# Two decoder layers for one token on one core: 256 more floats of W_q stay in SBUF for layer two

## The chip, the core and the metric

The kernel runs on one core of one Trainium2 chip. The metric is device time in microseconds (us) of one execution. Three executions of the kernel before gave a median of 729.7 us (729.67 to 729.95).

## The reference

Two identical layers share their weights and caches. Each layer is attention followed by a gated MLP, with a layer norm ahead of each and a residual sum behind each. There are 4 batches, one query token, a width of 640, 32 heads of 128, and of each cache the last W = 1024 positions count.

```python
W = min(4096, max(256, Sk // 4))
q = (x @ wq).reshape(B, Sq, Hq, Dh).transpose(0, 2, 1, 3)
k = k_cache[:, :, Sk - W:, :]
v = v_cache[:, :, Sk - W:, :]
scores = jnp.einsum("bhqd,bhkd->bhqk", q, k) * (Dh ** -0.5)
o = jnp.einsum("bhqk,bhkd->bhqd", softmax(scores), v)
# ... attention: o.transpose(0, 2, 1, 3).reshape(B, Sq, Hq * Dh) @ wo
gate, up = x @ W_gate, x @ W_up          # 640 -> 1728
h = gate * (gate > 0) * up               # then h @ W_down, 1728 -> 640
# ...
x = x + attention(layernorm(x)); x = x + mlp(layernorm(x))   # twice
```

All data are float32. One layer reads 10.5 MB of W_q, 67 MB of K, 67 MB of V, 10.5 MB of W_o and 13.3 MB of MLP weights.

## The kernel before

The weights and caches are laid out in HBM as three long rows of 128 partitions, in the order in which the program reads them: `heads` (the heads that are streamed in each layer), `kept` (five heads, which layer one reads last and which stay in SBUF for layer two), and `mlp`. A fourth, `limbs`, holds 512 floats of one head's V (head 17) cut into short pieces of 5 or 2 or 1 rows, which fill partitions of a small region at the end of SBUF.

SBUF holds the tile `store` of 50304 floats a partition and the tile `first_q`, which holds the first HELD = 4608 floats of `heads` (the beginning of W_q) from the start to the end, so that layer two does not load them again. A list `plan`, written out before anything is issued, says for each load the layer, the row, the range and the place in `store`. `load()` walks along it on SyncE (SP): a load is issued as soon as every column of its place is free, and nothing behind it goes first. `done` marks columns free after the matmuls that read them. So the order of the loads is fixed by `plan`, and the moment at which one may start is set by TensorE (PE), which reads the place's last data. Under each `dma_start` the wait stands on SP's own queue.

The stages, and what sets the order in each:

- Layer one's attention goes over groups of four heads (the last ones of three and two): `query` multiplies by W_q, `query_turned` transposes into `qT`, `scores` accumulates K products in the PSUM tile `ps`, `softmax` makes `probs`, `values` accumulates V products in `po` with weights in the two tiles `pT`, `project` adds W_o products to `y`. Loads there have up to MOST = 16064 floats a partition, and go round in three thirds of `store`.
- At the end of layer one's attention the kept heads fill `store` up to FRONT = 47360. Layer one's MLP has to pass through a small ring: what is left behind FRONT, plus three ranges of kept data that are parked elsewhere for a while: AHEAD (1088 floats of W_q, parked in free columns of `probs` and in the two `pT`), BACK (1728 floats of V, parked in `ps`, in columns 128 to 511 of `po` and in the tile of `y`), AWAY (1280 more floats of V, parked in `pp` and the two PSUM banks `m`). The ring has 7040 floats in seven places.
- `forward` is the MLP: `gate(j)` for the four parts 3, 0, 1, 2 (accumulating in one of the two halves of the PSUM tile `pp`), `gated(j)` (Relu on ScalarE (ACT), the product on VectorE (DVE)), `hidden(j)` (a transpose) and `down(j)` into `y`. In layer one `fill` and `busy` issue matmuls on the identity into `po[:, :P]` whose result nobody reads; they stand among the real ones.
- Layer two starts with the kept heads, then streams `heads` from column HELD on, first into the ring's places and then into larger and larger ones, and ends with `mlp` in pieces that grow smaller.

The layer norm is `normalized` (mean, subtraction, sum of squares with its ACT `accum_out`, transpose into `xT`) and `deviation` (four small matmuls for the variance, square root on ACT, reciprocal on DVE). `query_out` applies the reciprocal to the query's product on DVE.

Loads are L229 (`first_q`), L242 (rows of 128 partitions) and L238 (limbs). All products with loaded data are issued by the helper `product` (L276). L358 is `busy`, L365 is `fill`, L374 the sums over partitions in `mean`, L425 `query_out`, L605 and L606 `gated`.

Of the kernel before, what the change touches and what calls it, by code (L numbers as in the profile page):

```python
# [14 lines left out]
P = 128  # L15
# [44 lines left out]

HELD = 4608
STORE = 50304
FRONT = KEPT * 2 * (D + KV)


AHEAD = KEPT * D, KEPT * D + 1088
INSIDE = 864
BACK = FRONT - 2 * KV - 1728, FRONT - 2 * KV
AWAY = BACK[0] - 1280, BACK[0]
HOME = 12864  # L70
FIRST, MOST = 32128, 16064
LAP = 3 * MOST
SPLIT, PART = 17, 2048
LIMBS = [(half + i, 5, 0, 1536) for i in range(4) for half in (0, 32)] + [(i, 2, 1536, PART) for i in range(3)] + [(3, 1, 1536, PART), (7, 1, 1536, PART)]
RUNS = [(half, 20, 512 * s, 40 * s + 20 * (half > 0)) for s in range(3) for half in (0, 32)] + [(0, 8, 1536, 120)]
# [38 lines left out]
def decode_kernel(ctx: ExitStack, tc: tile.TileContext, x, source, out):  # L114
# [29 lines left out]
    def stretch(layer, lo, end, to):  # L144

        loads = []
        for hi in fewest(lo, end, -(-(end - lo) // MOST))[1]:
            if to + hi - lo > LAP:
                to = 0
            loads.append((lo, hi, to))  # L150
            to, lo = to + hi - lo, hi
        last = next(i for i, (lo, hi, _) in enumerate(loads) if lo < at_part("v", SPLIT) + KV - 512 <= hi)
        for i, (lo, hi, at) in enumerate(loads):
            if last - 3 < i <= last:
                half = (i - last + 1) * 6 + 1
                plan.extend((layer, "limbs", p, p + 1, STORE - PART) for p in range(max(half, 0), half + 6))
            put(layer, "heads", at, lo, hi)
        return to
# [19 lines left out]
    put(0, "heads", q_end, turn, *mid, heads_end)  # L178
    put(0, "kept", k0, k0, k1, v0, v0 + 6656, v1, v1 + KV, v1 + 7168, FRONT)
    put(0, "kept", 0, 0, len(HEADS[K0]) * D, KEPT * D)  # L180


    f, z, a, q, k = FRONT, STORE - D, AHEAD[0], AWAY[0], BACK[0]
    assert STORE - FRONT == 1280 + 1024 + D
    gu = [(z, D), (f, 1280), (f + 1280, 1024), (a, 1088), (k, 960), (k + 960, 768), (q, 1280)]
    gu_end = [(f, 1280), (f + 1280, 1024), (z, D), (a, D + 256)]
    wd = [(k, 960), (k + 960, D), (q, 1280), *gu_end, (k, D), (k + D, D)]
    lo = 0
    for to, n in gu + gu + gu_end + wd:
        put(0, "mlp", to, lo, lo + n)  # L190
        lo += n
    assert lo == MLP


    lo = HELD
    for to, n in (f, 1280), (f + 1280, 1024), (z, D), (a, 1088), (k, 1728):
        put(1, "heads", to, lo, lo + n)
        lo += n
    to = AHEAD[1]
    for n in 832, 1280, 1024, 2048, 3392:  # L200
        to = put(1, "heads", to, lo, lo + n)
        lo += n
# [12 lines left out]
    for lo, hi in (last, near(last + 12800)), (near(last + 12800), heads_end):  # L215
        to = put(1, "heads", to if to + hi - lo <= STORE else 0, lo, hi)
    cuts = [0, 7040, 12160, GU0 + 3 * GU, WD1 + WD, MLP - 4 * D, MLP - 2 * D, MLP - D, MLP - QUARTER, MLP]
    for lo, hi in zip(cuts, cuts[1:]):
# [32 lines left out]
    def place(layer, row, lo):  # L251
# [4 lines left out]
        if row == "kept" and layer:  # L256
            if AHEAD[0] <= lo < AHEAD[1]:
                i = lo - AHEAD[0] - INSIDE
                if i < 0:
                    return probs, 1024 + i, -i  # L260
                return pT[i // P], GAP + i % P, min(P - i % P, AHEAD[1] - lo)
            if BACK[0] <= lo < BACK[1]:
# [144 lines left out]

    def query(layer, g, spread=False):

# [12 lines left out]
        part_done(layer, "q", g, c * n, n)  # L422

    def query_out(g, rstd):
# [38 lines left out]
    def values(layer, g, last=False):  # L463
# [30 lines left out]
        if last:  # L494
# [4 lines left out]
            if layer == 0:  # L499
                nc.gpsimd.tensor_copy(pT[0][:, GAP:], store[:, AHEAD[0] + INSIDE:AHEAD[0] + INSIDE + P])  # L500
                rest = AHEAD[1] - AHEAD[0] - INSIDE - P
                nc.vector.tensor_copy(pT[1][:, GAP:GAP + rest], store[:, AHEAD[1] - rest:AHEAD[1]])
                free(*AHEAD)
# [31 lines left out]
    def attention(layer):  # L535
        gs = order[layer]
        rstd = deviation(normalized())
        table(AF.Exp)
        query(layer, gs[0], True)
        if layer:  # L540
            for t in pT:
                nc.gpsimd.memset(t, 0.0)
# [42 lines left out]
    def forward(layer):  # L585
# [35 lines left out]
        def down(j, last=False):  # L621
# [4 lines left out]
            for f in range(4 if j < 3 else 1):  # L626
# [108 lines left out]
```

## Time and profile before

| what | value |
|---|---|
| median of three executions | 729.7 us |
| profiled execution, its time | 729.74 us |
| its span (first to last instruction) | 727.9 us |
| read from HBM | 310.32 MB |
| mean rate of the DMA engines | 427 GB/s |
| PE busy | 450.0 us (62%) |
| DVE, ACT, POOL busy | 70.5, 54.5, 2.4 us |
| mean granted clock of PE | 0.815 of full speed |

The span is what the views show; around it lie 1.8 us. Layer one's attention runs to about 364 us, its MLP to about 395 us, layer two's attention to about 704 us. In a line of the page, `store<-in_heads` is a load that writes `store` from the row `heads`; `po<-store,pT` is a matmul that writes `po` and reads `store` and `pT`.

### The profile page before, as it was taken

To read this page: it belongs to the slowest core of one execution; us is meant where nothing else is said; L and a number is where in the kernel's file an instruction comes from. 1 tells how busy PE (TensorE), PEld (TensorE's weight loads), DVE (VectorE), ACT (ScalarE), POOL (GpSimd) and SP (SyncE) were. 2 spreads that over 40 slices of the span, in tenths; PEclk is the share of its full clock that TensorE was granted. 3 is DMA by queue.
4 is the path that set the end of the run, shared out by engine and by line. 5 is a ranking of instruction groups with operands and counts; after the bars stand their busy time and mean duration, and the time that the engine had idled before them with its cause. 6 is when DMAs were issued, how large, how long until landed. Compare 5 with 4: busy or idle time off the path is not lost.

```text
span 727.9 us, 8368 instructions
## 1 busy us (share of the span) xinstructions
PE 450.0 (62%) x3824; PEld 146.9 (20%) x3824; DVE 70.5 (10%) x217; ACT 54.5 (7%) x102; POOL 2.4 (0%) x14
## 2 busy tenths in 40 slices
PE   3546565654645574619868896475756556558576
PEld 1111111111111121103334241021211012102123
DVE  2010001000010000001111211000000010001011
ACT  2000000000000000000412210000000000000100
POOL 0000000000000000000000000000000000000000
PEclk9567888887777787759999999677777878769989
DMA  9999999999999999999999999999999999999997
GB/s 409 444 394 447 440 444 434 412 435 444 443 428 416 421 457 418 444 422 426 418 414 412 426 431 452 429 441 433 434 423 440 438 436 417 441 444 423 425 420 312
DMA packets 13442, 310.91 MB, mean 427 GB/s; under 512 B 1576, under 2 KB 1916, under 8 KB 7136
## 3 DMA queue, kind: packets, MB, share of 16 engines
q1 hardware_dynamic: 13392, 310.37, 99.2%
q8 instruction: 30, 0.49, 0.2%
q14 instruction: 4, 0.03, 0.0%
q10 hardware_dynamic: 16, 0.01, 0.0%
HBM read 310.32 MB, written 0.05 MB: 426 GB/s over the span
## 4 chain that ended last, share of the span: by engine, by line
DMA 77%; PE 20%; DVE 1%; issue 1%; SPq 1%; ACT 0%; DVEq 0%; ACTq 0%
DMA store<-in_heads 62%; DMA store<-in_kept 9%; PE ps L276 8%; DMA store<-in_mlp 6%; PE po L276 6%; PE m L276 2%; PE y L276 1%; PE pp L276 1%; PE pp L461 1%; PE po L490 0%; PE m L432 0%; SPq L238 0%; PE po L358 0%; PE m L521 0%; PE m L512 0%
## 5 line engine op out<-in xcount | busy, mean ns | idle before, releaser
L276 PE MATMUL po<-store,pT 128*16 128x512 f32 x1026 | 157.9, 711 | 120.9 <-DMA store<-in_heads 115.2
L276 PE MATMUL ps<-store,qT 128*4 128x512 f32 (+2 forms) x998 | 152.7, 698 | 101.0 <-DMA store<-in_heads 80.7
L276 PEld LDWEIGHTS po<-store,pT 128*16 128x16 f32 x1026 | 33.4, 109 | 229.5 <-DMA store<-in_heads 126.7
L276 PEld LDWEIGHTS ps<-store,qT 128*4 128x4 f32 x998 | 30.8, 94 | 204.3 <-DMA store<-in_heads 91.8
L457 ACT ACTIVATE probs<-ps,nm 128x1024 f32<-128x1024 f32 x17 | 18.9, 1113 | 334.6 <-DVE nm L453 334.6
L453 DVE TENSOR_REDUCE nm<-ps 128x1 f32<-128x1024 f32 x17 | 20.8, 1225 | 233.9 <-PE ps L276 233.9
L276 PE MATMUL m<-store,xT 128*32 128x512 f32 (+3 forms) x146 | 27.9, 580 | 20.8 <-DMA store<-in_heads 20.8
L276 PE MATMUL y<-store,oT 128*4 128x160 f32 x512 | 23.2, 313 | 10.2 <-DMA store<-in_heads 8.9
L508 ACT COPY gates<-po 128x512 f32<-128x512 f32 x16 | 9.4, 586 | 256.5 <-PE po L276 256.5
L276 PE MATMUL pp<-store,xT 128*32 128x256 f32 (+2 forms) x320 | 20.3, 351 | 9.2 <-DMA store<-in_mlp 4.7
L470 DVE COPY pT<-pp 128x32 f32<-128x32 f32 x64 | 10.3, 184 | 143.5 <-PE po L276 126.4
L461 PE MATMUL pp<-sel_sb,probs 128*128 128x128 f32 x144 | 21.3, 297 | 0.0
L461 PEld LDWEIGHTS pp<-sel_sb,probs 128*128 128x128 f32 x144 | 18.7, 156 | 0.0
L514 DVE RECIPROCAL r<-m 128x16 f32<-128x16 f32 x18 | 4.6, 257 | 123.5 <-PE m L512 123.5
L276 PEld LDWEIGHTS y<-store,oT 128*4 128x4 f32 x512 | 12.7, 89 | 18.4 <-DMA store<-in_heads 9.2
L425 DVE TENSOR_SCALAR gates<-m,rstd 128x512 f32<-128x512 f32 (+2 forms) x18 | 12.4, 690 | 27.1 <-PE m L276 27.1
L276 PEld LDWEIGHTS pp<-store,xT 128*32 128x32 f32 x320 | 10.4, 109 | 17.7 <-DMA store<-in_mlp 8.5
L432 PE MATMUL m<-sel_sb,gates 128*128 128x128 f32 x64 | 12.7, 324 | 0.3 <-DVE gates L425 0.3
L276 PEld LDWEIGHTS m<-store,xT 128*32 128x32 f32 x146 | 6.0, 113 | 32.4 <-DMA store<-in_heads 23.3
L521 PE MATMUL m<-sel_sb,gates 128*128 128x128 f32 x72 | 11.9, 288 | 0.8 <-DVE gates L497 0.8
L432 PEld LDWEIGHTS m<-sel_sb,gates 128*128 128x128 f32 x64 | 7.9, 160 | 19.7 <-issue 18.9
L276 PE MATMUL y<-store,gates 128*4 128x160 f32 (+2 forms) x188 | 9.8, 296 | 1.7 <-DMA store<-in_mlp 1.1
(91 smaller groups left out, 135.7 us busy)
## 6 DMA issues: line engine op xcount, KB each, us to landing
store<-in_heads SPq DMA_DIRECT2D x15, 7936.0 KB
store<-in_heads SPq DMA_DIRECT2D x6, 8032.0 KB
store<-in_heads SPq DMA_DIRECT2D x2, 8000.0 KB
store<-in_heads SPq DMA_DIRECT2D x1, 7872.0 KB
store<-in_heads SPq DMA_DIRECT2D x1, 7424.0 KB
store<-in_heads SPq DMA_DIRECT2D x1, 7360.0 KB
store<-in_heads SPq DMA_DIRECT2D x1, 7168.0 KB
store<-in_heads SPq DMA_DIRECT2D x1, 6400.0 KB
```

The source lines that it names most:

```text
L276: nc.tensor.matmul(out[:, a:z], by, t[rows, p:p + z - a], start=start and not a, stop=stop and z == n, **how)
L425: nc.vector.tensor_scalar(gates[:, :len(HEADS[g]) * P], qp.pop(g), rstd, SCALE, op0=ALU.mult, op1=ALU.mult)
L432: nc.tensor.transpose(qt[:, i], gates[:, i * P:(i + 1) * P], ident)
L453: nc.vector.tensor_reduce(nm[g], to.rearrange("p j n -> p (j n)"), axis=AX.X, op=ALU.max, negate=True)
L457: nc.scalar.activation(probs, sc.pop(g).rearrange("p j n -> p (j n)"), AF.Exp, bias=nm.pop(g), accum_out=sums[g])
L461: nc.tensor.transpose(pp[:, c // 4, c % 4 * P:c % 4 * P + P], probs[:, c * P:(c + 1) * P], ident)
L470: nc.vector.tensor_copy(to, pp.rearrange("p j (c x) -> p (j c) x", c=4)[:, :, i:P:32])
L508: nc.scalar.copy(gates, po)
L514: nc.vector.reciprocal(r[g], so.rearrange("p (b i) -> p i b", b=B)[:, :SIDE])
L521: nc.tensor.transpose(ot[:, 127 * b:127 * b + P], gates[:, b * P:(b + 1) * P], ident)
```

## The change

- HELD grows from 4608 to 4864 floats and `store` shrinks from 50304 to 50048. Layer two streams `heads` from 4864 on: 256 floats a partition less.
- Loads are at most 16000 floats (16064 before), and a third of `store` is 16000.
- The ring of layer one's MLP becomes 6848 floats in six places, of which one has 1408 floats; layer one's MLP is 23 loads instead of 27. Layer two's first loads of `heads` go into the ring in four pieces instead of five. Layer two's first two loads of `mlp` (7040 and 5120 floats) become one of 12160. AHEAD is 1152 floats; its last 32 are parked in `qT`, by a copy on GpSimd (POOL), and POOL then also clears `qT` in layer two.
- The limbs are 12 loads a layer instead of 13; two loads of one row become one of two rows.
- `gate(j)` accumulates in `pp[:, 0]` for the parts 3 and 1, and in columns 256 to 511 of `po` for the parts 0 and 2; in layer one these lie among the columns in which BACK is parked.
- At the start of each attention the first `query` now runs ahead of `deviation`: four of its five row blocks are multiplied, then come the variance's small matmuls, then the fifth block.
- In layer one's `down`, `busy` is issued in the first of the three large parts alone: 4 times instead of 10.

```diff
-HELD = 4608
-STORE = 50304
+HELD = 4864
+STORE = 50048
...
-FIRST, MOST = 32128, 16064
+FIRST, MOST = 32000, 16000
...
-LIMBS = [(half + i, 5, 0, 1536) for i in range(4) for half in (0, 32)] + [(i, 2, 1536, PART) for i in range(3)] + [(3, 1, 1536, PART), (7, 1, 1536, PART)]
+LIMBS = [(half + i, 5, 0, 1536) for i in range(4) for half in (0, 32)] + [(i, 2, 1536, PART) for i in range(4)]
...
-    gu = [(z, D), (f, 1280), (f + 1280, 1024), (a, 1088), (k, 960), (k + 960, 768), (q, 1280)]
+    gu = [(f, 1280), (f + 1280, 1408), (a, 1152), (k, 960), (k + 960, 768), (q, 1280)]
...
-    cuts = [0, 7040, 12160, GU0 + 3 * GU, ...
+    cuts = [0, 12160, GU0 + 3 * GU, ...
...
-    def query(layer, g, spread=False):
+    def query(layer, g, spread=False, between=None):
...
         part_done(layer, "q", g, 0, (KC - 1) * n)
+        value = between and between()
+        turn_of[0] ^= value is not None
         c = KC - 1
...
-        rstd = deviation(normalized())
+        ss = normalized()
+        rstd = query(layer, gs[0], True, lambda: deviation(ss))
         table(AF.Exp)
-        query(layer, gs[0], True)
         if layer:
-            for t in pT:
+            for t in qT, *pT:
                 nc.gpsimd.memset(t, 0.0)
...
+                lo = AHEAD[0] + INSIDE + 2 * P
+                nc.gpsimd.tensor_copy(qT[:, :AHEAD[1] - lo], store[:, lo:AHEAD[1]])
...
-            gus[j] = pp[:, j % 2, :2 * P]
+            gus[j] = pp[:, 0, :2 * P] if j % 2 else po[:, 2 * P:]
...
-                elif not (last and f > 1):
+                elif j == 0:
                     busy(1)
```

On SP, at layer one's MLP (a row is one or several loads; the number behind the name is partitions by floats). Before, the first twelve rows of it:

```order
L242 DMA store<-in_mlp 128x640
L242 DMA store<-in_mlp 128x1280
L242 DMA store<-in_mlp 128x1024
L242 DMA store<-in_mlp 128x1088
L242 DMA store<-in_mlp 128x960
L242 DMA store<-in_mlp 128x768
L242 DMA store<-in_mlp 128x1280
L242 DMA store<-in_mlp 128x640
L242 DMA store<-in_mlp 128x1280
L242 DMA store<-in_mlp 128x1024
L242 DMA store<-in_mlp 128x1088
L242 DMA store<-in_mlp 128x960
```

After, the same place on SP:

```order
L241 DMA store<-in_mlp 128x1280
L241 DMA store<-in_mlp 128x1408
L241 DMA store<-in_mlp 128x1152
L241 DMA store<-in_mlp 128x960
L241 DMA store<-in_mlp 128x768
L241 DMA store<-in_mlp 128x1280 x2
L241 DMA store<-in_mlp 128x1408
L241 DMA store<-in_mlp 128x1152
L241 DMA store<-in_mlp 128x960
```

The place of 640 floats is gone, and what it held is spread over the places beside it.

On PE, at the start of layer two (two sums over partitions for mean and variance, L374 before and L375 after, with the first query's products, which write `m` from parked and kept W_q). Before:

```order
L374 MATMUL m_124<-ones,sel_sb 32x1 x4
L365 MATMUL po<-sel_sb 128x128
L374 MATMUL m_123<-ones,sel_sb 32x1 x4
L276 MATMUL m_124<-probs,xT 32x384 x2
L276 MATMUL m_124<-probs,xT 32x96
L276 MATMUL m_124<-pT_113,xT 32x128
L276 MATMUL m_124<-pT_114,xT 32x96
L276 MATMUL m_124<-store,xT 32x64
L276 MATMUL m_124<-store,xT 32x384
L276 MATMUL m_124<-store,xT 32x96 x4
```

After, on PE:

```order
L375 MATMUL m_123<-ones,sel_sb 32x1 x4
L366 MATMUL po<-sel_sb 128x128
L277 MATMUL m_124<-probs,xT 32x384 x2
L277 MATMUL m_124<-probs,xT 32x96
L277 MATMUL m_124<-pT_113,xT 32x128
L277 MATMUL m_124<-pT_114,xT 32x128
L277 MATMUL m_124<-qT,xT 32x32
L277 MATMUL m_124<-store,xT 32x384
L375 MATMUL m_123<-ones,sel_sb 32x1 x4
L277 MATMUL m_124<-store,xT 32x96 x4
```

The variance's four matmuls moved behind seven of the query's eleven, and one of the products now reads `qT`.

On PE, in layer two's MLP (the gate products; L617 before and L623 after is `hidden(3)`). Before:

```order
L276 MATMUL pp<-store,xT 32x128 x15
L374 MATMUL m_124<-ones,sel_sb 32x1 x4
L404 MATMUL y<-probs,sel_sb 128x160
L276 MATMUL pp<-store,xT 32x256 x20
L617 MATMUL m_123<-sel_sb,gates 64x4 x4
L276 MATMUL pp<-store,xT 32x256 x40
```

After, on PE:

```order
L277 MATMUL pp<-store,xT 32x128 x15
L375 MATMUL m_124<-ones,sel_sb 32x1 x4
L405 MATMUL y<-probs,sel_sb 128x160
L277 MATMUL po<-store,xT 32x256 x20
L623 MATMUL m_123<-sel_sb,gates 64x4 x4
L277 MATMUL pp<-store,xT 32x256 x20
L277 MATMUL po<-store,xT 32x256 x20
```

Neighbouring parts now write different PSUM tiles.

More of the change, by code (lines that the diff above doesn't have):

```diff
@@ L55 @@
 MLP = WD1 + 3 * WD
-HELD = 4608
-STORE = 50304
+HELD = 4864
+STORE = 50048
 FRONT = KEPT * 2 * (D + KV)
-AHEAD = KEPT * D, KEPT * D + 1088
+AHEAD = KEPT * D, KEPT * D + 1152
 INSIDE = 864
@@ L153, in stretch @@
         for i, (lo, hi, at) in enumerate(loads):
-            if last - 3 < i <= last:
-                half = (i - last + 1) * 6 + 1
-                plan.extend((layer, "limbs", p, p + 1, STORE - PART) for p in range(max(half, 0), half + 6))
+            if last - 2 < i <= last:
+                half = (i - last + 1) * 6
+                plan.extend((layer, "limbs", p, p + 1, STORE - PART) for p in range(half, half + 6))
             put(layer, "heads", at, lo, hi)
@@ L178, in decode_kernel @@
     put(0, "heads", q_end, turn, *mid, heads_end)
-    put(0, "kept", k0, k0, k1, v0, v0 + 6656, v1, v1 + KV, v1 + 7168, FRONT)
+    put(0, "kept", k0, k0, k1, v0, v0 + 6144, v1, v1 + KV, v1 + 7168, FRONT)
     put(0, "kept", 0, 0, len(HEADS[K0]) * D, KEPT * D)
-    f, z, a, q, k = FRONT, STORE - D, AHEAD[0], AWAY[0], BACK[0]
-    assert STORE - FRONT == 1280 + 1024 + D
-    gu = [(z, D), (f, 1280), (f + 1280, 1024), (a, 1088), (k, 960), (k + 960, 768), (q, 1280)]
-    gu_end = [(f, 1280), (f + 1280, 1024), (z, D), (a, D + 256)]
-    wd = [(k, 960), (k + 960, D), (q, 1280), *gu_end, (k, D), (k + D, D)]
+    f, a, q, k = FRONT, AHEAD[0], AWAY[0], BACK[0]
+    assert STORE - FRONT == 1280 + 1408
+    gu = [(f, 1280), (f + 1280, 1408), (a, 1152), (k, 960), (k + 960, 768), (q, 1280)]
+    wd = [*gu[:4], (k + 960, 704), (q, 1280), *gu[:4], (k + 960, D)]
     lo = 0
-    for to, n in gu + gu + gu_end + wd:
+    for to, n in gu + gu + wd:
         put(0, "mlp", to, lo, lo + n)
@@ L195, in decode_kernel @@
     lo = HELD
-    for to, n in (f, 1280), (f + 1280, 1024), (z, D), (a, 1088), (k, 1728):
+    for to, n in (f, 1280), (f + 1280, 1408), (a, 1152), (k, 1728):
         put(1, "heads", to, lo, lo + n)
@@ L199, in decode_kernel @@
     to = AHEAD[1]
-    for n in 832, 1280, 1024, 2048, 3392:
+    for n in 768, 1280, 1024, 2048, 3392:
         to = put(1, "heads", to, lo, lo + n)
@@ L216, in decode_kernel @@
         to = put(1, "heads", to if to + hi - lo <= STORE else 0, lo, hi)
-    cuts = [0, 7040, 12160, GU0 + 3 * GU, WD1 + WD, MLP - 4 * D, MLP - 2 * D, MLP - D, MLP - QUARTER, MLP]
+    cuts = [0, 12160, GU0 + 3 * GU, WD1 + WD, MLP - 4 * D, MLP - 2 * D, MLP - D, MLP - QUARTER, MLP]
     for lo, hi in zip(cuts, cuts[1:]):
@@ L260, in place @@
                     return probs, 1024 + i, -i
-                return pT[i // P], GAP + i % P, min(P - i % P, AHEAD[1] - lo)
+                if i < 2 * P:
+                    return pT[i // P], GAP + i % P, P - i % P
+                return qT, i - 2 * P, AHEAD[1] - lo
             if BACK[0] <= lo < BACK[1]:
@@ L422, in query @@
         part_done(layer, "q", g, c * n, n)
+        return value
     def query_out(g, rstd):
@@ L499, in values @@
             if layer == 0:
-                nc.gpsimd.tensor_copy(pT[0][:, GAP:], store[:, AHEAD[0] + INSIDE:AHEAD[0] + INSIDE + P])
-                rest = AHEAD[1] - AHEAD[0] - INSIDE - P
-                nc.vector.tensor_copy(pT[1][:, GAP:GAP + rest], store[:, AHEAD[1] - rest:AHEAD[1]])
+                for i, on in enumerate([nc.gpsimd, nc.vector]):
+                    lo = AHEAD[0] + INSIDE + P * i
+                    on.tensor_copy(pT[i][:, GAP:], store[:, lo:lo + P])
                 free(*AHEAD)
```

## The prediction

> **What bounds the kernel now.** I read the page's DMA lines first.
>
> ```profile
> DMA  9999999999999999999999999999999999999997
> DMA packets 13442, 310.91 MB, mean 427 GB/s; under 512 B 1576, under 2 KB 1916, under 8 KB 7136
> q1 hardware_dynamic: 13392, 310.37, 99.2%
> DMA 77%; PE 20%; DVE 1%; issue 1%; SPq 1%; ACT 0%; DVEq 0%; ACTq 0%
> ```
>
> SP's queue keeps the 16 DMA engines at work for 99.2% of the span, and only the last of 40 slices shows a 7. The chain (fourth line) is DMA for 77%. Its 20% of PE cannot be time in which DMA stood, because less than 1% is left for that: PE's share matters only where it would delay a load so long that the queue runs empty. So the time is bytes over rate, a start and a tail. Next, the rate by stage (columns: stretch and length, busy time and count on PE, PEld, DVE, ACT, POOL, then granted clock, DMA share, GB/s).
>
> ```profile
> 3.00:236.00 233.00, 126.50 (x891) 37.14 (x891) 18.46 (x52) 12.94 (x22) 0.00 (x0) 0.78 1.01 435
> 236.00:346.00 110.00, 64.75 (x555) 19.95 (x555) 9.73 (x30) 5.37 (x9) 0.00 (x0) 0.78 0.99 429
> 346.00:406.00 60.00, 49.16 (x594) 22.22 (x595) 8.72 (x33) 15.69 (x33) 0.66 (x3) 1.00 1.01 412
> 406.00:722.00 316.00, 206.99 (x1735) 66.34 (x1733) 31.00 (x97) 19.77 (x37) 0.00 (x0) 0.82 1.00 432
> ```
>
> The one slow stretch is the passage from layer one's MLP through the ring into layer two: 412 GB/s against 432 behind it, at a DMA share of 1.01. What it issues, with the largest group and one of the smallest:
>
> ```profile
> DMA packets 5853, 24.74 MB, mean 412 GB/s; under 512 B 654, under 2 KB 654, under 8 KB 5514
> store<-in_mlp SPq DMA_DIRECT2D x7, 640.0 KB
> store<-in_heads SPq DMA_DIRECT2D x1, 320.0 KB
> ```
>
> In all, 38 loads (27 of `mlp`, 11 of `heads`). At 432 GB/s the 24.74 MB take 57.3 us, so this stretch loses 2.7 us. Last, the tail: the chain's end, and the DMA engines just before it.
>
> ```profile
> 693.76 30.76 DMA store<-in_mlp
> 724.52 0.04 issue
> 724.57 0.45 PE y L276 x6
> 725.02 0.16 PE m L276 x2
> 725.21 0.33 DVE first_q L677
> ```
> ```profile
> 721.00:722.00 1.00, 0.29 (x11) 0.26 (x14) 0.00 (x0) 0.00 (x0) 0.00 (x0) 1.00 0.95 383
> 722.00:723.00 1.00, 0.98 (x32) 0.53 (x20) 0.00 (x0) 0.00 (x0) 0.00 (x0) 1.00 0.78 302
> 723.00:724.00 1.00, 0.57 (x20) 0.41 (x24) 0.33 (x1) 0.00 (x0) 0.00 (x0) 1.00 0.45 168
> 724.00:725.00 1.00, 0.86 (x24) 0.28 (x14) 0.00 (x0) 0.00 (x0) 0.00 (x0) 1.00 0.13 33
> ```
>
> The last load lands at 724.5; behind it come two short steps and the store of the output, which the change leaves alone. The share falls over more than 2 us: the 16 engines do not finish together, so whatever burdens the one that ends last counts in full.
>
> **The change, part by part.** *Bytes.* 256 floats x 4 B x 128 partitions = 131,072 B fewer. At 432 GB/s that is 0.30 us. It leaves a queue that is never empty, so nothing hides it: -0.30.
>
> *Fewer full-width loads.* Layer one's MLP has 4 fewer, the entry to layer two 1, layer two's MLP 1: six. The price of one load is bounded by the slow stretch: 2.7 us over 38 loads is 72 ns each if everything lost there is the cost of a load, and nothing if all of it is engines running dry. Two rows show that some of it is dry time:
>
> ```profile
> 392.00:394.00 2.00, 2.00 (x31) 0.80 (x30) 0.00 (x0) 0.00 (x0) 0.00 (x0) 1.00 1.00 376
> 400.00:402.00 2.00, 1.97 (x21) 0.54 (x24) 0.44 (x2) 0.00 (x0) 0.00 (x0) 1.00 0.98 386
> ```
>
> These two dips are worth (432-376)/432 x 2 + (432-386)/432 x 2 = 0.5 us of the 2.7. The steady deficit of the rest (some 58 ns a load) is nearer the upper end, so I take 50 ns: six loads give -0.30, between 0 and -0.43.
>
> *Limbs.* Same bytes, one load fewer in each layer: between 0 and 2 x 72 = 0.14 us; I take -0.1. The Trainium skill ("DMA: Bandwidth & Descriptors", "Why a DMA increments its semaphore by 16 and not by 1") says that a load of k rows runs on the lowest-numbered k engines; then the two one-row loads, both on the lowest engine, become one on the lowest two, and the lowest engine, the likely last to finish, is spared 2 x 2048 B at 27 GB/s, an estimate of 0.15 us. The sum by it would be 0.05 us lower; no run shown here tells which engine moved a packet.
>
> *PE's matmuls on the identity.* Ten `busy` become four, between these two and their like:
>
> ```profile
> 389.93 0.33 PE L358 MATMUL po<-sel_sb 128*128 128x128 f32 x1
> 394.22 0.33 PE L358 MATMUL po<-sel_sb 128*128 128x128 f32 x1
> ```
>
> Six times at most 0.33 us make up to 2.0 us of PE's time ahead of layer two. PE then waits for the same weights to land; the covering work is the queue, so 0 in the sum. If the queue does run dry there, this is what PE can give back.
>
> *Gates in two tiles.* At the end of layer two the waits for the other half of `pp` stand in brackets (idle time, and who ended it):
>
> ```profile
> 705.93 1.18 PE L276 MATMUL pp<-store,xT 128*32 128x128 f32 x27 [0.47 <-DVE xT L388]
> 708.54 2.37 PE L276 MATMUL pp<-store,xT 128*32 128x256 f32 x40 [0.81 <-DVE gates L606]
> 711.78 2.37 PE L276 MATMUL pp<-store,xT 128*32 128x256 f32 x40 [0.54 <-DVE probs L606]
> 715.02 2.37 PE L276 MATMUL pp<-store,xT 128*32 128x256 f32 x40 [0.87 <-DVE probs L606]
> 718.57 0.84 PE L276 MATMUL y<-store,probs 128*4 128x160 f32 x16 [1.19 <-DMA store<-in_mlp]
> ```
>
> 0.81 + 0.54 + 0.87 = 2.2 us of waits go, and PE waits 2.2 us longer at 718.57 for weights: 0 in the sum.
>
> *The merged load of 12160.* The gates may start only when all of it has landed. Behind it 13,760 floats a partition, 7.05 MB, remain; at this stage's 418 GB/s
>
> ```profile
> 690.00:722.00 32.00, 22.07 (x309) 9.79 (x312) 4.53 (x16) 2.76 (x9) 0.00 (x0) 0.89 0.98 418
> ```
>
> they take 16.9 us, so it lands near 707.6, 1.7 us after PE would start at 705.93. PE has 2.2 + 1.19 = 3.4 us in hand before 718.57, so 0. Without that cover it would be +1.7 - 1.19 = +0.5.
>
> *Query ahead of the variance.* At layer two's start:
>
> ```profile
> 396.57 0.34 DVE L388 STREAM_TRANSPOSE xT<-gates 128x160 f32<-128x160 f32 x1
> 397.06 0.24 PE L374 MATMUL m<-ones,sel_sb 128*32 128x1 f32 x8 [0.55 <-ACT gates L386]
> 397.43 0.26 ACT L394 ACTIVATE rstd<-m,ones 128x1 f32<-128x1 f32 x1 [0.42 <-PE m L374]
> 397.72 0.16 DVE L395 RECIPROCAL rstd<-rstd 128x1 f32<-128x1 f32 x1 [0.80 <-ACT rstd L394]
> 398.58 0.62 DVE L425 TENSOR_SCALAR gates<-m,rstd 128x384 f32<-128x384 f32 x1 [0.70 <-PE m L276]
> 398.09 0.36 POOL L542 MEMSET pT<- 128x140 f32 x2 [41.32 <-PE m L276]
> ```
>
> The products no longer wait for ACT's sum (`xT` is there at 396.9, some 0.2 us earlier), and the place they free, which the next load wants, is free as much earlier. The variance moves behind seven of eleven products, some 0.9 of the 1.5 us that they take up to 398.58; the root and the reciprocal (done at 397.88 before) follow it, so L425 moves from 398.58 to about 398.8, and the scores with it. Queued behind that are the loads that wait for scores, 0.2 us later, against up to 2.0 us that PE gained before: 0. At layer one's start the same shift lies under the first big load. POOL's two memsets of `pT` took 0.36 us; a third, of `qT`, ends before the transposed query is written there, behind L425: 0.
>
> *A shorter ring.* 6848 for 7040 floats: 192 x 512 B = 0.1 MB, 0.24 us less cover at 412 GB/s. While the queue holds more than that: 0; else the rival below.
>
> Sum: -0.30 - 0.30 - 0.10 = -0.7 us. The profiled execution's 729.74 (727.9 span and 1.8 around) becomes 729.0; it lies 0.04 above the median, so 729.0 is also my forecast of the median. Changes under 0.2% (1.5 us) are about what a measurement of this kernel cannot tell from none, and this one is such.
>
> **Rivals.** *The slow stretch heals* (faster). If the 2.7 us are mostly PE freeing the ring late, then PE's 2.0 us at its end and the waits gone from its gates return most of it: 0.3 + 0.1 + about 2 us, 727.3. For it: SP waits for PE throughout.
>
> ```profile
> SPq L242 <- PE pp L276: 11.1, 12, 2.5
> SPq L242 <- PE y L276: 10.1, 9, 4.6
> ```
>
> Against it: the DMA share stays at 1.01 there, so SP's waits are mostly time in which the queue still has work. Chance 0.14.
>
> *The ring is too short* (slower). Six coarser places are freed in steps of 1141 floats on average, not 1006, 135 x 512 B = 0.17 us later at 412 GB/s, and each turn has 0.24 us less cover. If no slack were left, 23 loads x 0.17 us + 3.8 turns x 0.24 us = 4.8 us; with half of them exposed, +2.4 - 0.7 = +1.7: 731.4. It decides once the slowest engine waits at a place, which takes lateness beyond what it still has queued. For it: the two dips. Against it: they are worth 0.5 us in 60. Chance 0.10.
>
> *PE becomes the bound at the end.* The two tiles do not free PE (another wait stands in the same place), and the load of 12160 costs its 0.5: 729.5. Chance 0.06.
>
> *It does less than it says.* A load costs nothing and the limbs neither; the bytes alone remain: 729.4. Against it: the steady deficit where loads are small. Chance 0.12.
>
> *Loads pay a fixed time.* If each issue put silence on the engines, the price would be that of the start, where SP issues at 0.73 and the first slice is empty:
>
> ```profile
> 0.00:1.00 1.00, 0.00 (x0) 0.00 (x0) 0.18 (x2) 0.00 (x0) 0.43 (x5) 1.00 0.00 0
> 1.00:2.00 1.00, 0.00 (x0) 0.00 (x0) 0.79 (x3) 0.00 (x0) 0.83 (x4) 1.00 1.07 231
> ```
>
> At some 0.5 us for each of 8 loads: 725.7. Thirty-eight loads that lost 2.7 us together speak against it; chance 0.01. The Trainium skill ("DMA: Bandwidth & Descriptors", "Anatomy of one DMA") gives a fixed 2.0 us for one DMA, which would be 16 us for eight; by the stretch above the trace does not agree for loads that overlap.
>
> **How the numbers follow.** My forecast has 0.57: 729.0, with 728.5 to 729.7 for it alone (all terms at their upper ends -0.9, or the bytes with late gates +0.0). With the two mild rivals it makes 0.75, and these three are all within 0.2%. The range reaches half way to the healed stretch (728.0) and to the short ring (730.3). Faster by over 0.2% is the healed stretch and the fixed time, 0.15; slower is the short ring, most of whose cases pass 731.2, 0.09; the remainder, 0.76, is no change that can be told.
>
> **What would show it.** Right: 310.19 MB read, the stretch from 346 to 406 a few GB/s above 412 with five fewer loads, the other stages as before, L606 gone as releaser of gate products, and the last DMA landing some 0.7 us sooner. Wrong: single slices in the ring well below 376 GB/s with SP waiting for PE (short ring); the ring's stretch at 425 or more (healed); PE at 718 no longer waiting for a load (PE bound).

## The result and the profile after

| | before | after |
|---|---|---|
| median of 22 executions each | 729.68 us | 731.49 us |
| where they lie | 18 of 22 from 729.4 to 730.1 | 16 of 22 from 730.1 to 732.4 |
| ratio after to before | | 1.0026, 95% interval 1.0019 to 1.0033 |
| profiled execution: time, span | 729.74, 727.9 us | 734.13, 732.4 us |

The kernel became slower, by 1.8 us in the median, and its executions scatter: from 729.95 to 734.57 us. One of before's 22 took 1176.73 us; nothing here shows why, and it moves neither the median nor the ratio. The profiled execution after is at the upper end: it shows larger losses than the median has, so it is read for their places.

One thing the changed kernel leaves out. Layer one's gates 0 and 2 now write columns 256 to 511 of `po`, where part of BACK is parked, and nothing saves it. Layer two copies these 256 columns back as V all the same, so it works there with gate values. What keeping them would cost, no run shows.

The page's lines on the clock, the rate and the traffic (40 slices of 18.3 us):

```profile
PEclk9988878787777787759989999687787878869889
GB/s 416 413 425 445 437 441 440 407 440 427 443 440 425 412 444 441 435 424 419 419 391 386 367 438 441 433 438 430 434 438 426 445 423 437 435 431 428 428 425 306
q1 hardware_dynamic: 12528, 310.24, 98.9%
HBM read 310.19 MB, written 0.05 MB: 424 GB/s over the span
```

The traffic is what was forecast, 310.19 MB, but SP's queue is busy for 98.9% in place of 99.2%. Three slices are low, 391, 386 and 367 GB/s, from 366 to 421 us. By stage, in the prediction's stretches (the last three columns are granted clock, DMA share, GB/s):

```profile
3.00:236.00 233.00, 125.62 (x897) 36.77 (x897) 18.46 (x52) 13.10 (x22) 0.00 (x0) 0.82 1.01 435
236.00:346.00 110.00, 65.20 (x555) 19.58 (x555) 9.27 (x30) 5.37 (x9) 0.21 (x1) 0.77 1.00 430
346.00:406.00 60.00, 47.60 (x550) 23.34 (x550) 8.79 (x32) 13.87 (x30) 0.75 (x4) 0.91 0.97 387
406.00:722.00 316.00, 206.59 (x1696) 66.24 (x1692) 30.54 (x94) 21.14 (x39) 0.00 (x0) 0.82 1.00 431
```

435, 430 and 431 GB/s are within 1 of before. Most of the 4.4 us between the two profiled executions is lost in the ring's stretch: 387 for 412 GB/s, at a DMA share of 0.97 for 1.01, which over 60 us is 60 x 25 / 432 = 3.5 us. The dip runs on to 408 us. The clock there, 1.00 before, is 0.91. In steps of 2 us:

```profile
374.00:376.00 2.00, 2.00 (x19) 1.36 (x19) 0.44 (x2) 0.37 (x1) 0.00 (x0) 0.50 1.01 413
380.00:382.00 2.00, 0.87 (x14) 0.28 (x6) 0.36 (x2) 0.00 (x0) 0.00 (x0) 1.00 0.94 321
400.00:402.00 2.00, 2.00 (x29) 1.40 (x24) 0.00 (x0) 0.00 (x0) 0.46 (x3) 0.50 0.94 372
402.00:404.00 2.00, 1.95 (x19) 1.00 (x18) 0.78 (x2) 1.75 (x3) 0.00 (x0) 0.89 0.42 83
404.00:406.00 2.00, 1.90 (x19) 0.50 (x21) 0.60 (x2) 0.00 (x0) 0.00 (x0) 1.00 0.78 261
406.00:408.00 2.00, 2.00 (x24) 0.54 (x20) 0.00 (x0) 0.00 (x0) 0.00 (x0) 1.00 0.92 288
```

The queue runs dry: a little at 380, and at 402 nearly wholly (share 0.42, 83 GB/s). Each time TensorE ran at half its clock just before (0.50 up to 378.5 and 402.4 us). The second place is layer two's start, where the query now stands ahead of the variance (timeline; in brackets the idle time before and who ended it):

```profile
399.77 0.86 PE L277 MATMUL m<-probs,xT 128*32 128x384 f32 x4 [0.48 <-ACT gates L387]
401.82 0.26 PE L375 MATMUL m<-ones,sel_sb 128*32 128x1 f32 x2
402.19 0.26 ACT L395 ACTIVATE rstd<-m,ones 128x1 f32<-128x1 f32 x1 [2.48 <-PE m L375]
402.76 0.62 DVE L429 TENSOR_SCALAR gates<-m,rstd 128x384 f32<-128x384 f32 x1
404.41 4.04 PE L277 MATMUL pp<-store,qT 128*4 128x512 f32 x36
```

The root starts 2.4 us after the query (402.19 - 399.77). In before, L425 waited 0.70 us for the query's product; now L429 has no wait left for PE and starts behind the reciprocal. Layer two's MLP shows the rest of the forecast order, and one new wait:

```profile
712.90 2.06 PE L277 MATMUL pp<-store,xT 128*32 128x128 f32 x27 [3.38 <-DMA store<-in_mlp]
726.19 1.27 PE L277 MATMUL y<-store,gates 128*4 128x160 f32 x32 [0.99 <-DMA store<-in_mlp]
```

The waits for L606 between the gates are gone, the load of 12160 is waited for (3.38 us), and PE has caught up at the end, where it waits for a load again (0.99 us).

Two causes were conceivable: the order at layer two's start, and the falls of the clock. Beside them stood the prediction's own rivals, the ring and the tail.

### The profile page after: what moved, and what is told of

It reads as the page before. It is cut to its first block, busy times and chain, and to the rows that moved or that the text cites. A ratio compares the mean times of both kernels' runs of the same rounds, so it can differ in the third digit from the quotient of the medians.

```text
span 732.4 us, 8352 instructions
## 1 busy us (share of the span) xinstructions
PE 451.2 (62%) x3822; PEld 149.0 (20%) x3822; DVE 70.6 (10%) x217; ACT 54.4 (7%) x102; POOL 2.7 (0%) x16
## 3 DMA queue, kind: packets, MB, share of 16 engines
q1 hardware_dynamic: 12528, 310.24, 98.9%
HBM read 310.19 MB, written 0.05 MB: 424 GB/s over the span
## 4 chain that ended last, share of the span: by engine, by line
DMA 77%; PE 21%; issue 1%; DVE 1%; ACT 0%; SPq 0%; DVEq 0%; ACTq 0%
DMA store<-in_heads 61%; PE ps L277 10%; DMA store<-in_mlp 8%; DMA store<-in_kept 8%; PE po L277 5%; PE m L277 2%; PE y L277 1%; PE pp L277 1%; PE m L436 1%; PE pp L465 0%; PE po L366 0%; PE m L525 0%; PE m L516 0%; DVE qT L439 0%; ACT m L585 0%
## 5 line engine op out<-in xcount | busy, mean ns | idle before, releaser
L277 PE MATMUL po<-store,pT 128*16 128x512 f32 (+2 forms) x1028 | 154.2, 703 | 127.8 <-DMA store<-in_heads 122.2
L277 PE MATMUL ps<-store,qT 128*4 128x512 f32 (+5 forms) x996 | 155.9, 698 | 105.5 <-DMA store<-in_heads 83.1
L465 PE MATMUL pp<-sel_sb,probs 128*128 128x128 f32 x144 | 19.5, 281 | 0.0
L465 PEld LDWEIGHTS pp<-sel_sb,probs 128*128 128x128 f32 x144 | 17.1, 146 | 0.0
L277 PE MATMUL po<-store,xT 128*32 128x256 f32 (+2 forms) x170 | 13.8, 392 | 4.5 <-DMA store<-in_mlp 4.5
L429 DVE TENSOR_SCALAR gates<-m,rstd 128x512 f32<-128x512 f32 (+2 forms) x18 | 12.4, 690 | 24.2 <-PE m L277 24.0
L277 PE MATMUL pp<-store,xT 128*32 128x256 f32 (+3 forms) x146 | 9.9, 411 | 3.8 <-DMA store<-in_mlp 3.4
L277 PE MATMUL m<-first_q,xT 128*32 128x512 f32 (+2 forms) x46 | 8.6, 718 | 4.8 <-DMA first_q<-in_heads 3.5
```

The source lines that it names most:

```text
L277: nc.tensor.matmul(out[:, a:z], by, t[rows, p:p + z - a], start=start and not a, stop=stop and z == n, **how)
L429: nc.vector.tensor_scalar(gates[:, :len(HEADS[g]) * P], qp.pop(g), rstd, SCALE, op0=ALU.mult, op1=ALU.mult)
L465: nc.tensor.transpose(pp[:, c // 4, c % 4 * P:c % 4 * P + P], probs[:, c * P:(c + 1) * P], ident)
```

## The experiments

The kernel before, run beside them, had medians of 729.49 to 729.60 us throughout. Every kernel with gates in `po` overwrites the 256 columns of parked V, as the changed kernel does; no instruction or byte is added or saved by it. Four edits make up most of the kernels.

```diff
 # "variance first": the order of before
-        ss = normalized()
-        rstd = query(layer, gs[0], True, lambda: deviation(ss))
+        rstd = deviation(normalized())
         table(AF.Exp)
+        query(layer, gs[0], True)
 # "halves": both gate tiles in pp, as before
-            gus[j] = pp[:, 0, :2 * P] if j % 2 else po[:, 2 * P:]
+            gus[j] = pp[:, j % 2, :2 * P]
 # "ten busy", as before
-                elif j == 0:
+                elif not (last and f > 1):
                     busy(1)
 # "split": the load of 12160 in two again
-    cuts = [0, 12160, GU0 + 3 * GU, ...
+    cuts = [0, 7040, 12160, GU0 + 3 * GU, ...
```

### Undoing TensorE's edits in the changed kernel

a1: variance first, halves and ten busy. The new ring, the loads and the limbs stay.

> The changed kernel with its three edits on PE undone (ten busy matmuls in layer one's down, gates in the two halves of pp, the variance ahead of the query), so that HELD, the ring, the loads and the limbs are all that differs from the kernel before. Theory clock (without its matmuls on the identity PE idles while it waits for loads, the granted clock falls to 0.5 around layer two's start, the ring is freed late and the queue runs dry): full clock from 346 to 406, 412 GB/s or a little more there, and 729.0 to 729.4, by the bytes and loads saved. Rival ring (six coarser places of 6848 floats are too short): still 731 to 732, with slices under 376 GB/s in the ring at full clock.

a2: ten busy alone.

> The changed kernel with busy issued ten times again in layer one's down. As in the changed kernel, the gates of parts 0 and 2 overwrite 256 columns of V that are parked in po. Theory clock: no fall of the clock at layer two's start, so the larger of the two dents (83, 261 and 288 GB/s from 402 to 408) goes: 729.3 to 730.3; a fall inside the gates near 372 may remain. Rival ring: no change, 731.5. Rival query order (the variance behind the products makes layer two's scores late): no change, 731.5.

a3: halves alone.

> The changed kernel with the gates in the two halves of pp again; busy four times and the query ahead of the variance, as changed. Theory clock, with the down part as the place that matters: still slow, 730.7 to 731.7, with the clock at full speed in the gates near 372 but falling near 399 in some executions. If the gates in two tiles were what lets PE idle (it runs ahead of the loads), this one returns to 729.0 to 729.7. Rival ring: 731.5.

a4: variance first alone.

> The changed kernel with the variance ahead of the first query again. Theory clock: the fall remains, but the place that the next load wants is freed a little later and the scores start a little sooner: within 0.4 of the changed kernel, 731.1 to 731.9. Rival query order: most of the loss goes, 729.5 or less. Rival ring: 731.5.

| | median (range), executions | ratio to before, 95% |
|---|---|---|
| a1 | 732.43 (730.95 to 733.25), 5 | 1.0032, 1.0019 to 1.0044 |
| a2 | 731.08 (729.98 to 732.75), 11 | 1.0019, 1.0011 to 1.0028 |
| a3 | 732.25 (731.94 to 733.70), 5 | 1.0038, 1.0025 to 1.0051 |
| a4 | 729.60 (728.97 to 730.09), 11 | 0.9997, 0.9988 to 1.0006 |

a4 takes the whole loss back and most of the scatter: the order of one query and the variance's matmuls is worth 1.9 us (731.49 - 729.60). Ten busy change little, halves make it no better. The clock theory's ranges for a1, a2 and a4 all failed; a4 lies 0.1 us above the range of "query order", a1 and a3 lie above every range. a1 is slow for another reason, at the end (its timeline in layer two's MLP, in the fastest of its five executions):

```profile
708.12 2.14 PE L277 MATMUL pp<-store,xT 128*32 128x128 f32 x27 [3.45 <-DMA store<-in_mlp]
711.78 3.42 PE L277 MATMUL pp<-store,xT 128*32 128x256 f32 x40 [0.42 <-DVE gates L612]
719.33 2.37 PE L277 MATMUL pp<-store,xT 128*32 128x256 f32 x40 [0.87 <-DVE probs L612]
```

PE waits 3.45 us for the merged load, then runs its first products at half the clock (3.42 us for what takes 2.37), and keeps the waits between halves: it waits for no load any more from there to the end, where before and after both still do: PE is the bound.

### The merged load, and the layer that counts

a5: a4 with split. a6: a1 with split.

> The changed kernel with the variance ahead of the query again (729.60 in that form) and with layer two's first load of mlp in two pieces, 7040 and 5120 floats, as before. Theory tail (the merged load holds up the gates at the end, but two tiles make up for it): no change, 729.3 to 729.8. If the merged load costs something in some executions, by the fall of the clock while PE waits for it, 729.0 to 729.3.

> All three PE edits undone, and the first load of mlp in two pieces: what is left of the change is HELD, the ring of six places, the sizes of the loads and the limbs. Theory tail (with gates in the halves of pp the merged load makes PE the bound at the end; the ring costs nothing): 729.0 to 729.7. Rival ring (six coarser places are too short): 731 or more, as with the merged load (732.4).

a7 and a8: the new order in one layer alone.

```diff
-        rstd = query(layer, gs[0], True, lambda: deviation(ss))
+        rstd = query(layer, gs[0], True, lambda: deviation(ss)) if layer == 0 else deviation(ss)   # a7; a8: layer == 1
         table(AF.Exp)
+        if layer:                                                                                # a8: if layer == 0
+            query(layer, gs[0], True)
```

> The changed kernel with the query ahead of the variance in layer one alone. Theory late start (in layer two the order delays the reciprocal, the scores and the loads that wait for them, while the ring is nearly empty): as with the variance ahead in both layers, 729.3 to 729.9. Rival clock phase (the order in layer one shifts PE's work against the clock's windows): as the changed kernel, 731 to 732.

> The changed kernel with the query ahead of the variance in layer two alone. Theory late start: as the changed kernel, 731 to 732, with L429 bound by the reciprocal in layer two and the first loads after the query some 0.5 to 0.9 us later than with the variance ahead. Rival clock phase: 729.3 to 729.9.

| | median (range), executions | ratio to before, 95% |
|---|---|---|
| a5 | 729.82 (729.23 to 732.89), 11 | 1.0009, 1.0001 to 1.0018 |
| a6 | 730.44 (729.98 to 733.16), 11 | 1.0017, 1.0008 to 1.0026 |
| a7 | 729.68 (729.09 to 734.25), 12 | 1.0009, 0.9996 to 1.0021 |
| a8 | 731.16 (729.44 to 733.29), 12 | 1.0023, 1.0013 to 1.0033 |

The merged load costs 2.0 us with halves (a1 against a6) and nothing with two tiles (a4 against a5): there the two tiles do the work that the prediction gave them. The order costs its time in layer two (a8); in layer one the median stays (a7), though two of its twelve executions are above 733. Both lie in the ranges of "late start"; a5 lies 0.02 us above its range, a6 in neither of its two. a6, the new ring with before's work on TensorE, is 0.8 us slower than before, not 0.7 faster. Its profile shows part of it in the ring's stretch, at a clock of 1.00: 408 for 412 GB/s, 60 x 4 / 432 = 0.6 us.

```profile
346.00:406.00 60.00, 48.46 (x588) 22.03 (x584) 7.88 (x29) 15.16 (x33) 0.75 (x4) 1.00 1.01 408
```

### The same edits on the old ring

Each of these is the kernel before with the opposite of the edits above: b3 the query ahead, b4 the load merged, b12 two tiles and four busy, b2 two tiles alone, b5 all of them. HELD, the ring, the limbs are those of before.

> The kernel before, with one part of the change alone: the query ahead of the variance, in both layers, on the old ring of 7040 floats. Theory 'query order': on the changed ring this order moved the scores of layer two from 4.93 us to 5.46 us after y, and the loads behind them by up to 0.86 us, and cost 1.5 to 1.9 us of the median (729.60 without it, 731.49 with it). If the order is enough by itself, this run lies at 730.2 to 731.3. Rival 'ring': the order does harm only where the ring has lost 192 floats; then 729.4 to 729.9.

> The kernel before, with one load alone changed: the first 12160 floats of the last MLP in one load in place of 7040 and 5120. Theory 'tail': layer two's gate(3) then waits 2 to 3.5 us for the longer load, and with the gates in the halves of pp TensorE doesn't catch up before the last load: 731.0 to 731.7, with out issued more than 1.5 us behind the last load. Rival: the wait is worked off before the end and a load's fixed cost (up to 0.07 us) is saved: 729.5 to 729.7.

> The kernel before, with two parts alone: `busy` 4 times in place of 10 and gates in two PSUM tiles (256 columns of layer two's parked V are overwritten by gates of layer one; no instruction more or less for it). Theory 'relief': TensorE held back loads in the stretch from 346 to 406 us, and what the two parts spare it (0.84 us between a6 and a4 on the changed ring, a merged load included) comes back here too: 728.7 to 729.2. Rival 'bytes alone': the ring is not held back by TensorE there and the end waits for the last load either way: 729.4 to 729.7.

> The changed kernel with the old ring: before, with the query ahead, two tiles (256 columns of layer two's parked V overwritten), `busy` 4 times and the merged load of 12160; what is left out of the change is HELD 4864, the six places of 6848 floats and the limbs. Theory 'query order': nearly all of the changed kernel's loss is in it: 730.7 to 731.6. Theory 'ring': the shorter ring makes the loss, and this run lies at 729.4 to 730.2.

> The kernel before with one part alone: gates in two PSUM tiles (256 columns of layer two's parked V are overwritten by gates of layer one, at no cost in time). With `busy` 4 times as well it was 730.31. If the fewer busy matmuls made that loss through the clock, this run lies at 729.3 to 729.7, and its clock holds 1.00 from 346 to 406 us; if the two tiles made it, at 730.1 to 730.5.

| | median (range), executions | ratio to before, 95% |
|---|---|---|
| b3 | 730.25 (729.68 to 731.36), 11 | 1.0011, 1.0002 to 1.0020 |
| b4 | 730.20 (729.77 to 731.93), 11 | 1.0013, 1.0004 to 1.0022 |
| b12 | 730.31 (729.59 to 730.90), 11 | 1.0010, 1.0001 to 1.0019 |
| b2 | 730.30 (729.77 to 730.68), 11 | 1.0010, 1.0001 to 1.0018 |
| b5 | 730.13 (729.60 to 732.47), 11 | 1.0011, 1.0002 to 1.0020 |

The theories contradict each other here: b3 lies at the lower end of "query order", b5 in the range of "ring", b2 where two tiles make the loss; b4 and b12 lie in neither range. The order alone costs 0.7 us on the old ring (b3). With two tiles and four busy it costs nothing there: b5, which adds the order and the merged load to b12, is 0.2 us faster than b12, while on the new ring the same order costs 1.9 (a4 against after). All of these edits together cost 0.6 us on the old ring (b5 against before) and 1.05 on the new one (after against a6), a difference within the scatter. So the order is dear on the new ring and not on the old one, with the other edits as they are in the changed kernel; that the new ring lacks the slack for it fits this, but no run shows slack by itself. "Relief" is refuted: two tiles (b2) and fewer busy (b12) give nothing back on the old ring, and two tiles alone cost 0.75 us, at a clock of 1.00, with a ring stretch of 408 GB/s for 412 in the profiled execution. Why is not settled. The parts don't add up: b3 and b2 lose 0.7 each, b5 holds both and loses 0.6.

### The order with TensorE's clock held

c1: the changed kernel with ten busy and 14 filling matmuls in layer one's gates, one ahead of the first product on each new load. c2: variance first and ten busy. c3: c1 with variance first.

```diff
                     lo = at + (c * groups + g) * 2 * n
+                    if layer == 0 and j < 3 and any(lo <= f < lo + 2 * n for f, *_ in held[0, "mlp"]):
+                        fill(1, pp[:, 1])
```

> The changed kernel with `busy` 10 times again and, in layer one's gates 0 to 2, one filling matmul ahead of the first product on each new load (14 in all, some 0.2 to 0.4 us each, where TensorE waits 0.24 to 1.1 us for a load). Theory 'clock': the falls to 0.5 between 372 and 402 us make the loss; the granted clock holds 1.00 there and the run lies at 729.8 to 730.6. Theory 'query order': the clock holds, and the time stays at 731.0 to 731.6, as with `busy` alone (731.08). If the clock falls all the same, this run tells nothing.

> The changed kernel with the variance ahead of the query again (729.60) and `busy` 10 times. It may beat both: theory 'clock': more busy matmuls hold the clock and nothing waits for them: 729.0 to 729.5. Rival 'busy costs': they hold back the places that loads wait for: 729.8 to 730.4.

> The one before with the 14 filling matmuls in layer one's gates as well. Theory 'clock': no fall between 366 and 406 us, 728.9 to 729.4, under both kernels. Rival: the 14 matmuls hold back releases by up to 0.4 us each time where the queue is short: 730.0 to 731.0.

| | median (range), executions | ratio to before, 95% |
|---|---|---|
| c1 | 732.21 (731.64 to 732.73), 5 | 1.0036, 1.0023 to 1.0049 |
| c3 | 730.76 (730.54 to 732.50), 11 | 1.0019, 1.0010 to 1.0027 |
| c2 | 730.00 (729.56 to 733.55), 12 | 1.0016, 1.0005 to 1.0028 |

c1 lies 0.6 us above the range of "query order"; c2 and c3 lie in those of their rivals. c1 and c3 are the cleanest pair: the clock holds 1.00 in both from 346 to 406 us, and `y` is finished at the same time (the first matmul behind its last product starts at 396.09 and 396.07; "the end of `y`" below is this moment). c3, then c1, at layer two's start:

```profile
398.25 0.26 ACT L395 ACTIVATE rstd<-m,ones 128x1 f32<-128x1 f32 x1 [0.42 <-PE m L375]
399.41 0.62 DVE L429 TENSOR_SCALAR gates<-m,rstd 128x384 f32<-128x384 f32 x1 [0.70 <-PE m L277]
399.85 0.35 SPq L241 DMA_DIRECT2D store<-in_heads  x1
401.00 5.33 PE L277 MATMUL pp<-store,qT 128*4 128x512 f32 x48
```
```profile
399.33 0.26 ACT L395 ACTIVATE rstd<-m,ones 128x1 f32<-128x1 f32 x1 [1.49 <-PE m L375]
399.65 1.05 PE L277 MATMUL m<-store,xT 128*32 128x256 f32 x10 [0.25 <-ACT rstd L395]
399.90 0.62 DVE L429 TENSOR_SCALAR gates<-m,rstd 128x384 f32<-128x384 f32 x1
400.73 0.33 SPq L241 DMA_DIRECT2D store<-in_heads  x1
401.55 5.33 PE L277 MATMUL pp<-store,qT 128*4 128x512 f32 x48
```

The root starts 1.08 us later, L429 0.49 (it now stands 0.11 behind the reciprocal, which ends at 399.79), the scores 0.55. The second query, which writes the PSUM bank that held the variance, now waits for the root to have read it (0.25 us, `<-ACT rstd`), and the load that its places are needed for is issued 0.88 us later. What that makes of the rate, before and behind `y` (c3, then c1):

```profile
366.00:396.00 30.00, 29.46 (x349) 15.62 (x343) 2.59 (x9) 3.02 (x8) 0.00 (x0) 1.00 1.01 406
396.00:410.00 14.00, 11.87 (x127) 5.03 (x123) 4.68 (x11) 5.40 (x11) 0.46 (x3) 1.00 0.99 386
```
```profile
366.00:396.00 30.00, 29.45 (x349) 15.68 (x343) 2.60 (x9) 3.02 (x8) 0.00 (x0) 1.00 1.01 408
396.00:410.00 14.00, 11.90 (x126) 4.63 (x118) 4.45 (x10) 5.40 (x11) 0.46 (x3) 1.00 0.97 353
```

14 x (386 - 353) / 432 = 1.07 us are lost, and the output is stored 1.13 us later:

```profile
726.43 0.36 SPq L640 DMA_DIRECT2D out_x<-probs  x1
```
```profile
727.56 0.36 SPq L640 DMA_DIRECT2D out_x<-probs  x1
```

By the medians the pair differs by 1.45 us. So the order's loss needs no fall of the clock at this place. It may need a ring that is already late. The 14 matmuls make `y` end 1.1 us later in both than in a4 (394.99). In after, a2, a3 and a8, the other profiles with this order on the new ring, it ends later than 396 us too, behind a fall of the clock. What the order costs there when `y` is on time, no profile shows.

On the old ring one does. Before, then b5 (profiled in the fastest of its eleven executions), where `y` ends at 395.24 and 395.14:

```profile
399.02 0.35 SPq L242 DMA_DIRECT2D store<-in_heads  x1
396.00:410.00 14.00, 12.12 (x128) 5.12 (x125) 4.38 (x10) 5.13 (x11) 0.36 (x2) 1.00 1.02 415
```
```profile
399.78 0.33 SPq L242 DMA_DIRECT2D store<-in_heads  x1
396.00:410.00 14.00, 12.13 (x116) 5.08 (x116) 4.38 (x10) 5.11 (x10) 0.37 (x2) 1.00 1.03 416
```

The load follows `y` by 3.78 us in before and 4.64 in b5, exactly as in c3 and c1. The same delay of 0.86 us costs no rate in b5, and 33 GB/s over 14 us in c1. Whether the shorter ring or its lateness makes that difference, these profiles don't separate.

c3 didn't beat before: the 14 matmuls cost 0.8 us (c3 against c2; 1.1 in c1 against a2). From 366 to 396 us c3 and c1 have 406 and 408 GB/s, where a4 has

```profile
366.00:396.00 30.00, 23.50 (x329) 11.93 (x320) 2.95 (x11) 3.32 (x9) 0.00 (x0) 1.00 1.02 413
396.00:410.00 14.00, 12.05 (x124) 5.01 (x127) 4.35 (x10) 5.11 (x10) 0.46 (x3) 1.00 1.02 411
```

Ten busy in place of four cost 0.4 us here (c2 against a4) and gained 0.4 in the pair a2 and after, so their sign is not told. The clock may matter apart from the order: c2's profiled execution (span 731.6 us, one of the three high ones of twelve) has the variance first and loses its time between 366 and 410 us, at a mean clock of 0.77.

```profile
366.00:396.00 30.00, 25.06 (x284) 13.51 (x278) 2.60 (x9) 3.02 (x8) 0.00 (x0) 0.77 0.97 382
396.00:410.00 14.00, 12.91 (x160) 5.29 (x151) 3.60 (x8) 4.19 (x9) 0.46 (x3) 1.00 0.96 356
```

### A place between

c4: the query ahead, with the variance behind its first row of blocks, not its fourth. c5: c4 with ten busy.

```diff
         for c in range(KC - 1):
             product(qp[g][32 * c:32 * c + 32], ...)
+            if c == 0:
+                value = between and between()
+                turn_of[0] ^= value is not None
         part_done(layer, "q", g, 0, (KC - 1) * n)
-        value = between and between()
-        turn_of[0] ^= value is not None
```

> The changed kernel with the variance behind the first of the query's five rows of blocks in place of the fourth. Theory 'place of the variance': Sqrt starts some 0.2 us later than with the variance first, in place of 1.08; the scores follow y by 4.9 to 5.05 us, and the run lies at 729.4 to 730.1. Rival 'the banks': the second query still waits for the bank that the variance has used, and the time stays at 731.0 to 731.6.

> The one before with `busy` 10 times, the pair of a2 (731.08) and c2 (730.00). Theory 'place of the variance': 729.7 to 730.3. Rival 'the banks': 730.8 to 731.3.

| | scores behind end of `y` | median (range), executions | ratio to before, 95% |
|---|---|---|---|
| c4 | 5.02 us | 730.58 (729.10 to 734.93), 11 | 1.0021, 1.0007 to 1.0035 |
| c5 | 5.02 us | 730.09 (729.27 to 732.42), 11 | 1.0011, 1.0002 to 1.0020 |

With the variance first the scores follow `y` by 4.93 us, with it behind four rows by 5.46. c5 lies where its theory put it, beside c2 (730.00) and not a2 (731.08). The root starts 0.62 us later than with the variance first (2.81 us behind `y` in c4, 2.19 in a4), not 0.2 as expected; the scores 0.09. c4 missed its range by 0.5 us: it lies between a4 and after, and scatters too widely to be told from after by its interval. No version here beats the kernel before; a4 equals it.

## Why the prediction was wrong, point by point

The forecast was 729.0 us within 728.0 to 730.3; the time is 731.49, 2.5 us more. Split by a4, which differs from the changed kernel in the order alone, 1.9 us of this are the order and 0.6 are savings that did not come. Split by a6, the new ring without the edits on TensorE, 1.44 us are missing there already (730.44), and the edits on TensorE with the merged load make 1.05.

- *Query ahead of the variance* is the step that failed: "0.2 us later, against up to 2.0 us that PE gained before: 0". By the medians of a4, c3 and c2 against after, c1 and a2 the term is +1.9, +1.45 and +1.1 us on the new ring, where the sum had 0. Three things in it were wrong. First, the delay: the sum moved the variance by 0.9 us and let the 0.70 us for which L425 waited cover nearly all of it. The root came 1.08 us later, 0.11 us passed between reciprocal and L429, so the cover was 0.59, and L429 came 0.49 us later, the scores 0.55. Second, the bank that the second query takes over from the variance, a new wait of 0.25 us, was not in the sum, and the load behind it came 0.88 us later. Third, the cover: the prediction had itself put TensorE's 2.0 us at 0, since PE then waits for the same weights, and yet set them against this delay. In c1 the delay was exposed, 1.07 us of lost rate and 1.13 us at the output. The gain on the other side hardly exists: the query started 0.06 us sooner (397.91 for 397.97), not 0.2; its row in after still names ACT's sum as what it waited for (`<-ACT gates L387`).
- *TensorE's 2.0 us of busy*: `y` ends at 394.98 with four busy (c4) and at 395.18 with ten (c5), so PE gained 0.2 us, not 2.0. In the medians, four for ten made 0.4 us less in one pair and 0.4 more in the other, about the 0 of the sum.
- *The rates of the queue* were read as "the DMA share stays at 1.01", so as slack. The two dips of before, 376 and 386 GB/s, were a warning that there might be little: one of them is this very place.
- *Bytes, loads, limbs*: -0.7 in the sum. The bytes are as forecast. In a4, which holds all three, the output is stored 0.34 us sooner than before in the profiled executions (725.05 for 725.39), but the medians are equal (729.60 and 729.59); no run tells the three terms apart. With before's order and work on TensorE (a6) it is +0.8.
- *The merged load and the two tiles*: right in mechanism, the cover held (a4 against a5). Without cover it cost 2.0 us on the new ring (a1 against a6) and 0.7 on the old one (b4), for 0.5 in the sum: the wait for the load was 3.45 us in a1, not 1.7, and TensorE's clock fell during it.
- *The ring is too short*, at 0.10, had the time (731.4) and its sign: single slices far under 376 GB/s with the queue dry. The time is partly luck, for the way to it was half right: places coming free later were exposed, but the experiment that takes the loss back (a4) changes the order and keeps the ring. What it had right is in a6, and in b5: the old ring with the same edits loses 0.6 us, not 1.8.
- Of what was to show it right, the bytes, the other stages' rates and L606 held. The ring's stretch fell instead of rising, and the last load landed at 729.0 in the profiled execution, for 724.5.

What stays open: why each edit on TensorE alone costs some 0.7 us on the old ring, how much of the order's loss hangs on a ring that is late already, and what decides whether an execution has the falls of the clock.

## What to carry to other kernels

Where a queue is fed through a small ring, a mean DMA share of 1.01 doesn't say that a step which releases a place has slack. Count the delay of every load behind a moved instruction, and look at single 2 us windows for dips before calling it hidden. Here the same 0.86 us cost nothing in one kernel and 1.1 us in another. A cover can't be spent if another line of the same sum has called it worthless. Moving a long-latency chain (sum, root, reciprocal, table load) behind matmuls to start these sooner pays only if the matmuls are the later of the two at the place where both meet; the 0.70 us wait at L425 said by how little they were. And after a bank is reused, ask who still reads it.

## What was not expected of the hardware

The granted clock falls to 0.50 for 3.41 us or a multiple of it, and comes back by itself. In after's profile it was 0.50 from 371.7 to 378.5, from 399.0 to 402.4 and from 713.0 to 716.5 us, and PE's products took up to 1.8 times as long: the 27 gate products behind the wait at the end took 2.06 and 2.14 us in after and a1, and 1.18 us in a4. a4's clock fell later, at 709.2 us, so there the next 40 products are slow, 3.60 us for 2.37:

```profile
708.01 1.18 PE L277 MATMUL pp<-store,xT 128*32 128x128 f32 x27 [2.38 <-DMA store<-in_mlp]
710.09 3.60 PE L277 MATMUL po<-store,xT 128*32 128x256 f32 x40
```

The Trainium skill ("TensorE: Matmul & The Clock Gate", "Part 1: The HAM clock gate (the "warmup" mystery)") gives a window of 3413 ns that runs free of the kernel, and a half clock after at least one idle window. The lengths of the falls fit that window, once and twice in the ring's stretch; that it starts elsewhere in each execution would fit the scatter, but no run shows it. The idle gaps in the ring's stretch were shorter than a window, though: the longest wait ahead of the fall at 399 was 1.64 us. In the 3.41 us ahead of each of the two falls there PE was busy for 1.82 and 1.60 us (the first number behind the length).

```profile
397.56 0.46 PE L277 MATMUL y<-store,gates 128*4 128x160 f32 x8 [1.64 <-DMA store<-in_mlp]
368.30:371.71 3.41, 1.82 (x31) 0.71 (x27) 0.01 (x1) 0.00 (x0) 0.00 (x0) 1.00 1.02 397
395.60:399.01 3.41, 1.60 (x28) 0.78 (x20) 0.41 (x2) 0.29 (x1) 0.00 (x0) 1.00 0.98 387
```

So in this trace the clock fell behind stretches in which PE was idle for about half the time, not for all of it. A fall is not always paid: b12's profile has a mean clock of 0.89 from 366 to 396 us, as after's has, and its 730.56 us lie 0.25 above its median; a7 and c2, at 0.77 there, were profiled at 733.1 and 733.5 us, 3.4 and 3.5 us above their medians. With the 14 filling matmuls it stayed at 1.00 in this stretch (c1, c3), at a price of 0.8 to 1.1 us; in before's and a4's profiles it did so without them.
